# Batch 0's kv products on 64-row by 128-column TensorE tiles, and f32 warm-up products

## The chip, the cores and the metric

The kernel runs on one core of one Trainium2 chip. The metric is the device time of one execution in microseconds. The engines are TensorE (PE, with PEld for its weight loads), VectorE (DVE), ScalarE (ACT), GpSimd (POOL) and SyncE (SP). Each engine takes its instructions in the order of its own queue and waits at an instruction until its semaphores are met. SP issues the plain loads and stores; POOL issues the loads that cast f32 to bf16.

## The reference, cut to what matters

```python
# q, k, v: (8 batches, 8 heads, 576 rows, 64)
q_s = softmax(q, over the 64 columns)
k_s = softmax(k, over the 576 rows)
kv  = einsum('bhsd,bhse->bhde', k_s, v)        # 64 x 64 for each head
attn = einsum('bhsd,bhde->bhse', q_s, kv)
x = attn, heads side by side                    # (4608, 512)
h = x @ w_in                                    # (4608, 2048)
s = sin(alpha * h)
out = (h + s * s / (alpha + 1e-9)) @ w_out      # (4608, 512)
```

The kernel takes exp(k) without dividing it; a column of ones beside v gives the sum of each column of exp(k) in the same product, and kv is divided by that sum once.

## The kernel before, in words

The 4608 rows of x are handled in nine slices of 512 columns of xT (x transposed, bf16). A slice t needs the attention of a batch; then 16 steps h (four products of 128x128 weights by 512 columns each, `mm_h`, L261), each followed by a sine (ACT, L267), a square (ACT, POOL or DVE by a list of letters, L269 to L273) and a sum (DVE, L277) that gives g; then 64 products with w_out (`mm_o`, L281). The order on every engine is written out by hand.

Heads lie in SBUF in this way: the 128 partitions hold two halves e of 64 rows; a head is h = 2*ii + x inside a half, so `ii` chooses a pair of heads and `x` one of the pair. `kv_mm` (L162 to L175) makes kv for a pair: for each of nine j, each x and each e one product with 64 rows, 64 weight columns (exp(k) of one head) and 65 moving columns (v of that head and its column of ones), so 36 products per pair, in four TensorE quarters. The result for the two heads x lies in the two halves of the partitions of `kvp`, one PSUM bank per e. `kv_norm` (L177 to L184) takes the reciprocal of the sums (L182, 128x2) and multiplies (L183, 128x128 for one pair, 128x256 for two) into `kbd`. `attn_x` (L211) multiplies kv with the transposed q.

The opening is the part that the change touches (L367 to L408). Its orders are:

- PE: seven warm-up products (`warm_up(7)`, L372: bf16 identity by 512 columns of `qe`, result never read), eight transposes of q for pair 0 into `tp0`, two warm-up products, the 36 kv products of pair 0, one warm-up product, the transpose of alpha, eight transposes of q for pair 1, `attn_x` of pair 0, the 36 kv products of pair 1, three products of h, `attn_x` of pair 1 (into `lp`), five products of h, and then the steps of slice 0, whose first waits for a part of w_in.
- ACT: exp of q pair 0 in two halves, exp of k pair 0, exp of q pair 1 in two halves, the cast of v pair 0 (`vb`), the copy of `tp0` into `qT`, exp of k pair 1, the copy of alpha, two copies into xT (L396), one more (L405), a load of the sine table (L406), and then the sines.
- DVE: sums, reciprocal and product for q of pair 0 and pair 1 (L362 to L364), the kv norm of pair 0, two casts of v pair 1 (L331), the copy of the second transposes into `qT` (L391), the kv norm of pair 1, the reciprocal of alpha, one copy into xT (L405), and then the sums L277.
- SP loads q, k and v of batch 0 without waiting. POOL issues two parts of v, eight loads of w_in (L107) and two of w_out (L110) one after another, and waits for nothing that PE does.

Later loads are tied to this order. In slice 0, after the sum of step 6, DVE writes one element into the tile of q (L443) and SP then loads the first half of q of batch 1 (L444). After steps 8 and 10 POOL issues two loads of w_out. After step 12 the second half of q, and then k and v of batch 1 (L452) follow. POOL issues the last part of w_out once k of batch 1 has landed. In the middle of the w_out products of slice 0 PE makes kv of batch 1: pair 0 (39.18 us) and pair 1 (42.65 us); in between a DVE write (L514) lets SP load a small part of q (`q8`, L515) and all of batch 2 (L98).

`late_q8` (L534) uses the kv of batches 0 and 1 once more at step 15 of slice 1.

Of the kernel before, what the change touches and what calls it, by code (L numbers as in the profile page):

```python
# [15 lines left out]
F32 = mybir.dt.float32  # L16
BF16 = mybir.dt.bfloat16
AX = mybir.ActivationFunctionType
ALU = mybir.AluOpType
# [4 lines left out]
def kernel(  # L24
# [14 lines left out]
    nc = tc.nc  # L39
    ctx.enter_context(nc.allow_non_contiguous_dma(reason="layout"))  # L40
    B, H, S, D = q.shape
# [3 lines left out]
    J = 9  # L45
    P = S // J
# [8 lines left out]
    singles = ctx.enter_context(tc.tile_pool(name="singles", bufs=1))  # L55
# [3 lines left out]
    small = ctx.enter_context(tc.tile_pool(name="small", bufs=2))  # L59
# [6 lines left out]
    ident = singles.tile([128, 128], F32, name="ident")  # L66
    identb = singles.tile([128, 128], BF16, name="identb")
# [4 lines left out]
    alpha_rows = singles.tile([nN, 128], F32, name="alpha_rows")  # L72
    alpha_sb = singles.tile([128, nN], F32, name="alpha_sb")
    inva_sb = singles.tile([128, nN], F32, name="inva_sb")
    kbd = [singles.tile([128, 2, 2, D], BF16, name=f"kbd{n}") for n in range(2)]
    vb = [singles.tile([128, J, 4 * 65], BF16, name=f"vb{n}") for n in range(2)]

# [7 lines left out]
    staged = {}  # L85
# [27 lines left out]
    A = {}  # L113
# [10 lines left out]
    def exp_half(name, b, ii, j1=J, j0=0):  # L124
        if (name + "e", b) not in A:
            A[name + "e", b] = att2.tile([128, J, 4 * D], BF16, name=name + "e")
        exp_to(A[name + "e", b][:, j0:j1], staged[name, b][:, :, j0:j1], (ii,))
# [34 lines left out]
    def kv_mm(b, ii, pool, split=False):  # L162

        if ii == 0 or split:
            A["kvp", b] = pool.tile([128, 2, 512], F32, name="kvp", tag="a")
        kvp, ke, vt = A["kvp", b], A["ke", b], vb[b % 2]
        for j in range(J):
            for x in range(2):
                h = 2 * ii + x
                for e in range(2):  # L170
                    r = slice(64 * e, 64 * e + 64)
                    nc.tensor.matmul(kvp[64 * x:64 * x + 64, e, ii * 65:(ii + 1) * 65],  # L172
                                     ke[r, j, h * 64:(h + 1) * 64],
                                     vt[r, j, h * 65:(h + 1) * 65],
                                     start=(j == 0), stop=(j == J - 1))  # L175

    def kv_norm(b, i0=0, i1=2):  # L177

        kt, m = kbd[b % 2], i1 - i0
        kvr = small.tile([128, 2, 2], F32, name="kvr")[:, :, 0:m]  # L180
        src = A["kvp", b][:, :, i0 * 65:i1 * 65].rearrange("p e (ii c) -> p e ii c", ii=m)
        nc.vector.reciprocal(kvr, src[:, :, :, D])  # L182
        nc.vector.tensor_tensor(kt[:, :, i0:i1], src[:, :, :, 0:D],  # L183
                                kvr.unsqueeze(3).to_broadcast([128, 2, m, D]), op=ALU.mult)  # L184
# [26 lines left out]
    def attn_x(b, ii, j0, j1, outs):  # L211

        for e in range(2):
            for x in range(2):
                r = slice(64 * x, 64 * x + 64)
                nc.tensor.matmul(outs[x][64 * e:64 * e + 64], kbd[b % 2][r, e, ii],  # L216
                                 A["qT", b][r, ii, j0:j1, e * 64:(e + 1) * 64], start=True, stop=True)

    def x_cols(b, j0, j1):
# [11 lines left out]
    def last_j(b, xn):  # L231

        for ii in range(2):
            attn_x(b, ii, J - 1, J, [xn[:, x, ii * P:(ii + 1) * P] for x in range(2)])
# [12 lines left out]
    def bank(kind):  # L247

        if kind == "k":
            return ps_k.tile([128, 2, MF], F32, name="kvp", tag="a")[:, 0]  # L250
        pool = {"a": lambda: ps_h[0], "b": lambda: ps_h[1], "l": lambda: ps_l, "o": lambda: ps_o[0], "p": lambda: ps_o[1]}[kind]()
        return pool.tile([128, MF], F32, name={"l": "lp", "o": "op", "p": "op"}.get(kind, "hp"), tag=kind)
# [69 lines left out]
    ps_k = ES.enter_context(tc.tile_pool(name="ps_k", bufs=1, space=PSUM, reuse_waits="tile"))  # L322

    tp0 = ps_h[0].tile([128, 8, 128], BF16, name="tp", tag="a")
    warm = ps_h[0].tile([128, 4, 128], F32, name="warm", tag="a")
# [19 lines left out]

    def warm_up(n):

        for _ in range(n):
            nc.tensor.matmul(warm, identb, A["qe", 0][:, 0:4, 0:128], start=True, stop=True)  # L349

# [4 lines left out]
    def norm_q0(ii):  # L357

        part = qs0[:, 0:8, 2 * ii:2 * ii + 2]
        src = qe0[:, 0:8, ii * 128:(ii + 1) * 128].rearrange("p j (x d) -> p j x d", x=2)  # L360
        for j0 in (0, 4):
            nc.vector.tensor_reduce(part[:, j0:j0 + 4], src[:, j0:j0 + 4], axis=AXL.X, op=ALU.add)  # L362
        nc.vector.reciprocal(part, part)
        nc.vector.tensor_tensor(qn0[:, ii, 0:8].rearrange("p j (x d) -> p j x d", x=2), src,  # L364
                                part.unsqueeze(3).to_broadcast([128, 8, 2, D]), op=ALU.mult)
# [3 lines left out]
    exp_half("k", 0, 0)  # L369
    for j0 in (0, 4):  # L370
        exp_half("q", 0, 1, j0 + 4, j0)
    warm_up(7)  # L372
    norm_q0(0)
    norm_q0(1)
    q_tile(0)
# [1 line left out]
    cast_v0(0, 0, 9, ACT_CP)  # L377
    ACT_CP(A["qT", 0][:, 0, 0:8], tp0)
    exp_half("k", 0, 1)
    warm_up(2)  # L380
    kv_mm(0, 0, ps_k, split=True)
    warm_up(1)
    tpa = warm[:, 0, 0:nN]
    nc.tensor.transpose(tpa, alpha_rows, ident[0:nN, 0:nN])
    kv_norm(0, 0, 1)
    tp1 = ps_l.tile([128, 8, 128], BF16, name="tp", tag="l")
    q_transpose_ii(0, 1, 0, 8, tp1)
    ACT_CP(alpha_sb, tpa)
# [3 lines left out]

    xp = [bank("b") for _ in range(2)]
    attn_x(0, 0, 0, 8, xp)
    for x in range(2):
        ACT_CP(xT[:, 2 * x, 0:MF], xp[x])  # L396
    kv_mm(0, 1, ps_k, split=True)
    kv_norm(0, 1, 2)
    nc.vector.reciprocal(inva_sb, alpha_sb)
    for ni, ki in ((0, 0), (1, 0), (0, 1)):  # L400
        mm_h(0, ni, ki, ki + 1)
    xp = [bank("l") for _ in range(2)]
    attn_x(0, 1, 0, 8, xp)
    for x in range(2):
        (ACT_CP, DVE_CP)[x](xT[:, 2 * x + 1, 0:MF], xp[x])  # L405
# [32 lines left out]
    with ES:  # L438
# [70 lines left out]
        take(os, 10)  # L509
        kv_mm(1, 0, ps_k, split=True)  # L510
        kv_norm(1, 0, 1)
        transpose_q1(1, DVE_CP)
        for b in range(2):
# [20 lines left out]
        def late_q8(ni):  # L534
            if ni == 11:
                tp = ps_k.tile([128, 2, 2, 128], BF16, name="tp", tag="a")
                for b in range(2):
                    for ii in range(2):
                        nc.tensor.transpose(tp[:, ii, b], A["qe", 1][:, J - 2 + b, ii * 128:(ii + 1) * 128], identb)
                DVE_CP(A["qT", 1][:, :, J - 2:J], tp)  # L540
            elif ni == 15:
                xp = ps_k.tile([128, 2, 512], F32, name="xp", tag="a")
                for ii in range(2):
                    for b in range(2):
                        for e in range(2):
                            for x in range(2):
                                r, c = slice(64 * x, 64 * x + 64), (2 * ii + b) * P
                                nc.tensor.matmul(xp[64 * e:64 * e + 64, x, c:c + P], kbd[b][r, e, ii],
                                                 A["qT", 1][r, ii, J - 2 + b, e * 64:(e + 1) * 64],
                                                 start=True, stop=True)  # L550
                DVE_CP(xT[:, :, 16 * P:18 * P].rearrange("p (x i) n -> p x i n", x=2),
                       xp[:, :, 0:4 * P].rearrange("p x (i n) -> p x i n", i=2))

        for ni in range(nN):
            h_slot(1, ni, SQ[ni], lag)
            flush(lag, 1)
            late_q8(ni)
# [34 lines left out]
    for ii in range(2):  # L592
        xp = [bank("ab"[ii]) for _ in range(2)]
# [29 lines left out]
    for ni in range(nN):  # L623
# [4 lines left out]
        elif ni in (9, 13):  # L628
            ii = ni // 12
# [3 lines left out]
    for t in range(3, nT):  # L633
        b = t + 1 if t + 1 < B else None
# [74 lines left out]
```

## Time and profile before

| | |
|---|---|
| median of 3 runs | 283.23 us (282.95 to 283.6) |
| profiled execution | 282.79 us, span 281.0 us |
| PE busy | 267.7 us (95%) |
| ACT, DVE, POOL busy | 223.8, 185.5, 81.3 us |
| first product of PE | 4.98 us |
| PE's wait for w_in in the opening ends | 14.87 us |
| PE's wait for v of batch 1 ends | 42.65 us |

The span is the profiled part of the execution; 1.8 us of it lie around the span. Times in the text are microseconds from the start of the span. In a line of the timeline the first number is the start, the second the length of the whole group, then come engine, source line, operation, output and inputs, tile and form, the count, and in brackets how long the engine had been idle before and what ended that.

### The profile page before, as it was taken

Reading aid. Unit: us, or ns where it says so; the run is one execution under the profiler, and the core shown is the slowest. Engines: PE = TensorE matmul, PEld = TensorE weight load, DVE = VectorE, ACT = ScalarE, POOL = GpSimd, SP = SyncE. Lnnn points to the kernel's source line nnn. Section 1 sums busy time; section 2 is a strip of 40 time slices with the busy share of each in tenths; the row PEclk is TensorE's granted clock in tenths of the full one; section 3 lists DMA queues with packets and bytes.
Section 4 is the critical chain, followed back from the end, with each engine's and each line's share of the span. In section 5 each row is a group of like instructions: output and inputs, shape, how many; then the busy total and the mean of one; then the engine's idle time right before and its main releaser. Section 6 shows DMA issues by size and latency. Waiting matters only on the chain.

```text
span 281.0 us, 4925 instructions
## 1 busy us (share of the span) xinstructions
PE 267.7 (95%) x1890; PEld 124.0 (44%) x1919; DVE 185.5 (66%) x279; ACT 223.8 (80%) x322; POOL 81.3 (29%) x77
## 2 busy tenths in 40 slices
PE   2899989999999999999999999999999999999994
PEld 1444444444443444444444444444444444444443
DVE  3968776899878767766776677577775555555412
ACT  5899458999588999899989998999877777777400
POOL 2968121777667460205003500350000000000000
PEclk9999999999999999999999999999999999999999
DMA  7999999997599039712991199125011111111143
GB/s 263 299 194 232 278 307 319 361 343 253 120 229 399 2 81 334 290 37 48 267 383 45 37 263 392 38 50 124 8 29 40 37 37 37 40 41 42 40 106 75
DMA packets 39320, 45.82 MB, mean 163 GB/s; under 512 B 17008, under 2 KB 22656, under 8 KB 39296
## 3 DMA queue, kind: packets, MB, share of 16 engines
q1 hardware_dynamic: 33392, 40.58, 46.9%
q0 software_dynamic: 5744, 4.79, 10.3%
q8 instruction: 15, 0.25, 0.3%
q10 hardware_dynamic: 160, 0.13, 0.2%
q14 instruction: 9, 0.07, 0.1%
HBM read 36.71 MB, written 9.44 MB: 164 GB/s over the span
## 4 chain that ended last, share of the span: by engine, by line
PE 85%; DMA 8%; POOL 2%; issue 1%; SPq 1%; ACT 1%; DVE 1%; ACTq 0%
PE op L281 38%; PE hp L261 38%; DMA st_v<-in_v_dram 4%; DMA win<-in_moe_w_in_dram 2%; PE lp L261 2%; PE kvp L172 2%; DMA st_k<-in_k_dram 2%; PE op L261 1%; PE op L679 1%; POOL s L271 1%; PE kvp L261 1%; PE hp L216 1%; PE xp L216 1%; POOL st_v L306 1%; DVE g L277 1%
## 5 line engine op out<-in xcount | busy, mean ns | idle before, releaser
L277 DVE SCALAR_TENSOR_TENSOR g<-s,inva_sb,hp 128x512 bf16<-128x512 f32 x128 | 94.5, 746 | 58.7 <-ACT s L269 53.3
L261 PE MATMUL hp<-xT,win 128*128 128x512 bf16 x506 | 127.7, 379 | 0.6 <-PE lp L216 0.2
L281 PE MATMUL op<-wout,g 128*128 128x512 bf16 x478 | 121.0, 379 | 1.6 <-issue 1.1
L267 ACT ACTIVATE s<-hp,alpha_sb 128x512 f32<-128x512 f32 x128 | 86.1, 682 | 22.3 <-PE hp L261 21.0
L261 PEld LDWEIGHTS <-win 128*128 128x128 bf16 x576 | 55.7, 98 | 67.8 <-DMA win<-in_moe_w_in_dram 1.2
L281 PEld LDWEIGHTS <-g 128*128 128x128 bf16 x560 | 53.4, 98 | 64.8 <-issue 2.3
L269 ACT ACTIVATE s<-s 128x512 f32<-128x512 f32 x112 | 70.5, 630 | 3.5
L271 POOL TENSOR_TENSOR s<-s 128x512 f32<-128x512 f32 x29 | 30.1, 1053 | 17.6 <-ACT s L267 11.3
L151 POOL TENSOR_TENSOR qn<-qe,qs 128x1152 bf16<-128x1152 bf16 x11 | 23.2, 2127 | 29.5 <-DVE qs L145 24.4
L293 DVE COPY o<-op 128x512 f32<-128x512 f32 (+2 forms) x33 | 21.8, 661 | 10.2 <-PE op L281 7.9
L136 POOL CAST vb<-st_v 128x1152 bf16<-128x1152 f32 x12 | 14.7, 1257 | 45.6 <-DMA st_v<-in_v_dram 45.6
L117 ACT ACTIVATE qe<-st_q 128x1152 bf16<-128x1152 f32 (+2 forms) x18 | 17.7, 1025 | 6.1 <-DMA st_q<-in_q_dram 6.0
L117 ACT ACTIVATE ke<-st_k 128x1152 bf16<-128x1152 f32 x16 | 17.9, 1151 | 3.2 <-DMA st_k<-in_k_dram 3.2
L144 DVE TENSOR_REDUCE qs<-qe 128x36 f32<-128x2304 bf16 x5 | 12.8, 2551 | 8.3 <-ACT qe L117 8.3
L117 ACT ACT_TABLE_LOAD x7 | 9.0, 1283 | 0.8 <-PEq L693 0.7
L172 PE MATMUL kvp<-vb,ke 64*64 64x65 bf16 x576 | 6.9, 194 | 2.2 <-ACT vb L470 1.5
L349 PE MATMUL warm<-qe,identb 128*128 128x512 bf16 x10 | 4.1, 554 | 5.0 <-ACT qe L117 5.0
L281 PE MATMUL hp<-wout,g 128*128 128x512 bf16 x31 | 8.6, 379 | 0.1
L172 PEld LDWEIGHTS <-ke 64*64 64x64 bf16 x576 | 6.0, 106 | 6.1 <-issue 3.4
L281 PE MATMUL lp<-wout,g 128*128 128x512 bf16 x30 | 8.4, 379 | 0.2 <-issue 0.2
L261 PE MATMUL lp<-xT,win 128*128 128x512 bf16 x30 | 7.5, 379 | 0.1
L229 DVE CAST xT<-xp 128x1024 bf16<-128x1024 f32 (+1 forms) x7 | 7.4, 1065 | 0.0
(89 smaller groups left out, 135.8 us busy)
## 6 DMA issues: line engine op xcount, KB each, us to landing
out_dram<-o SPq DMA_DIRECT2D x70, 128.0 KB, 2.4
st_q<-in_q_dram SPq DMA_DIRECT2D x6, 1152.0 KB, 6.3
st_k<-in_k_dram SPq DMA_DIRECT2D x6, 1152.0 KB, 8.6
st_v<-in_v_dram SPq DMA_DIRECT2D x6, 1152.0 KB, 11.3
st_k<-in_k_dram SPq DMA_DIRECT2D x4, 576.0 KB, 8.1
st_q<-in_q_dram SPq DMA_DIRECT2D x4, 512.0 KB, 6.0
st_v<-in_v_dram SPq DMA_DIRECT2D x3, 576.0 KB, 10.0
wout<-in_moe_w_out_dram POOLq DMA_DIRECT2D x3, 512.0 KB, 12.7
```

Of the source, the lines that this page charges most:

```text
L117: nc.scalar.activation(dst[:, :, ii * 128:(ii + 1) * 128].rearrange("p j (x d) -> p x j d", x=2), src[:, ii::2], AX.Exp)
L136: engs[ii](vv[:, 2 * ii:2 * ii + 2, :, 0:D], staged["v", b][:, ii::2])
L144: nc.vector.tensor_reduce(qs, A["qe", b].rearrange("p j (i d) -> p j i d", i=4), axis=AXL.X, op=ALU.add)
L151: engs[ii % len(engs)].tensor_tensor(qn[:, ii, 0:j1].rearrange("p j (x d) -> p j x d", x=2), qe[:, ii], part.unsqueeze(3).to_broadcast([12 ...
L172: nc.tensor.matmul(kvp[64 * x:64 * x + 64, e, ii * 65:(ii + 1) * 65], ke[r, j, h * 64:(h + 1) * 64], vt[r, j, h * 65:(h + 1) * 65], start= ...
L261: nc.tensor.matmul(hp, win[:, KO[k], ni * 128:(ni + 1) * 128], xT[:, KO[k], t * MF % NX:t * MF % NX + MF], start=(k == 0), stop=(k == 3))
L267: nc.scalar.activation(s, hp, AX.Sin, scale=alpha_sb[:, ni:ni + 1])
L269: nc.scalar.activation(s, s, AX.Square)
L271: nc.gpsimd.tensor_tensor(s, s, s, op=ALU.mult)
L277: nc.vector.scalar_tensor_tensor(G[t][:, ni], in0=s, scalar=inva_sb[:, ni:ni + 1], in1=hp, op0=ALU.mult, op1=ALU.add)
L281: nc.tensor.matmul(acc, G[t][:, ni, j * 128:(j + 1) * 128], wout[:, ni, :], start=(ni == 0), stop=(ni == nN - 1))
L293: eng(o[:, cols], acc)
```

## The change

Three things are changed, all for batch 0:

- The kv products of a pair are made by `kv0_mm`: for each j and e one product with 64 rows, all 128 weight columns of the pair, and 130 moving columns (both heads' v and ones). That is 18 products for a pair; the blocks of one head's k with the other head's v are made too and not used.
- The norm `kv0_norm` takes one column of sums per e (128x2) and multiplies 128 x (2 e, 2 blocks, 64) into a new tile `kv0`, from which `attn_x` and `late_q8` read the blocks that they need through `kv_of`.
- The warm-up products have the f32 identity as weights and the staged f32 q as moving operand, of n columns. They wait for the load of q and the identity in place of exp(q). The first seven become four of 512 columns, the two become one of 256, and the one becomes one of 128.

```diff
+    kv0 = singles.tile([128, 2, 2, 2, D], BF16, name="kv0")
...
+    def kv0_mm(ii):
+
+        A["kvp", 0] = ps_k.tile([128, 2, 512], F32, name="kvp", tag="a")
+        for j in range(J):
+            for e in range(2):
+                r = slice(64 * e, 64 * e + 64)
+                nc.tensor.matmul(A["kvp", 0][:, e, 0:130], A["ke", 0][r, j, ii * 128:(ii + 1) * 128],
+                                 vb[0][r, j, ii * 130:(ii + 1) * 130], start=(j == 0), stop=(j == J - 1))
+
+    def kv0_norm(ii):
+
+        kvr = small.tile([128, 2], F32, name="kvr0")
+        src = A["kvp", 0][:, :, 0:130].rearrange("p e (x c) -> p e x c", x=2)
+        nc.vector.reciprocal(kvr, src[:, :, 0, D])
+        nc.vector.tensor_tensor(kv0[:, :, ii], src[:, :, :, 0:D],
+                                kvr.unsqueeze(2).unsqueeze(3).to_broadcast([128, 2, 2, D]), op=ALU.mult)
+
+    def kv_of(b, x, e, ii):
+        r = slice(64 * x, 64 * x + 64)
+        return kbd[b % 2][r, e, ii] if b else kv0[r, e, ii, x]
...
-                nc.tensor.matmul(outs[x][64 * e:64 * e + 64], kbd[b % 2][r, e, ii],
+                nc.tensor.matmul(outs[x][64 * e:64 * e + 64], kv_of(b, x, e, ii),
                                  A["qT", b][r, ii, j0:j1, e * 64:(e + 1) * 64], start=True, stop=True)
...
     def warm_up(n):
 
-        for _ in range(n):
-            nc.tensor.matmul(warm, identb, A["qe", 0][:, 0:4, 0:128], start=True, stop=True)
+        nc.tensor.matmul(warm.rearrange("p a b -> p (a b)")[:, 0:n], ident,
+                         staged["q", 0][:, 0, 0:8].rearrange("p j d -> p (j d)")[:, 0:n], start=True, stop=True)
...
-    warm_up(7)
+    for _ in range(4):
+        warm_up(512)
     norm_q0(0)
     norm_q0(1)
     q_tile(0)
...
-    warm_up(2)
-    kv_mm(0, 0, ps_k, split=True)
-    warm_up(1)
+    warm_up(256)
+    kv0_mm(0)
+    warm_up(128)
     tpa = warm[:, 0, 0:nN]
     nc.tensor.transpose(tpa, alpha_rows, ident[0:nN, 0:nN])
-    kv_norm(0, 0, 1)
+    kv0_norm(0)
...
-    kv_mm(0, 1, ps_k, split=True)
-    kv_norm(0, 1, 2)
+    kv0_mm(1)
+    kv0_norm(1)
...
-                                nc.tensor.matmul(xp[64 * e:64 * e + 64, x, c:c + P], kbd[b][r, e, ii],
+                                nc.tensor.matmul(xp[64 * e:64 * e + 64, x, c:c + P], kv_of(b, x, e, ii),
```

## The prediction

> **What bounds the kernel now.** I read the chain of waits first, up to 46 us (columns: start, length, what):
>
> ```profile
> 8.90 5.92 DMA win<-in_moe_w_in_dram
> ...
> 14.87 1.90 PE hp L261 x8
> ...
> 29.41 12.43 DMA st_v<-in_v_dram
> ...
> 41.86 0.75 ACT vb L470
> ...
> 42.65 0.48 PE kvp L172 x32
> ```
>
> PE waits for a load twice: for w_in until 14.87, for v of batch 1 until 41.84 (cast, then product at 42.65). From there on the chain is PE almost without a break. So an opening that is quicker gains nothing by itself, and one that is later by d costs d less what the second wait swallows. The timeline of PE gives the room at both:
>
> ```profile
> 4.98 3.15 PE L349 MATMUL warm<-qe,identb 128*128 128x512 bf16 x7 [4.98 <-ACT qe L117]
> 7.92 0.87 PE L199 MATMUL tp<-identb,qn 128*128 128x128 bf16 x8
> 8.63 0.59 PE L349 MATMUL warm<-qe,identb 128*128 128x512 bf16 x2
> 9.72 0.48 PE L172 MATMUL kvp<-vb,ke 64*64 64x65 bf16 x36 [0.50 <-ACT vb L331]
> 10.45 0.23 PE L384 MATMUL warm<-ident,alpha_rows 16*128 16x16 f32 x1
> 13.20 0.41 PE L216 MATMUL lp<-qT,kbd 64*64 64x512 bf16 x4
> ...
> 39.18 0.48 PE L172 MATMUL kvp<-vb,ke 64*64 64x65 bf16 x36 [0.22 <-ACT vb L470]
> ...
> 42.65 0.48 PE L172 MATMUL kvp<-vb,ke 64*64 64x65 bf16 x36 [1.24 <-ACT vb L470]
> ```
>
> At 14.87 there is no room: five products of h begin at 13.77 and, at 0.216 each, end at 14.85, and w_in lands at 14.82. Between 14.87 and 39 PE runs with no gap. At 39.18 it waits 0.22 and at 42.65 1.24, so 1.46 us of lateness disappear there. The rows also show the clock. The granted clock reads 1.00 throughout, yet the weight loads of the first seven products start 0.43 apart (0.833 ns per column) and the eight transposes take 0.107 each, while the two products at 8.63 are 0.21 apart (0.42 ns per column). PE reaches full speed at about 8.6, 3.6 us after its first product.
>
> Third, the windows (DMA share is the next to last column):
>
> ```profile
> 27.00:28.00 1.00, 1.00 (x6) 0.49 (x5) 0.81 (x3) 1.00 (x3) 0.65 (x2) 1.00 1.14 291
> 28.00:29.00 1.00, 1.00 (x7) 0.42 (x5) 1.00 (x3) 0.98 (x2) 0.97 (x1) 1.00 1.17 252
> ...
> 40.00:41.00 1.00, 0.95 (x7) 0.34 (x5) 0.97 (x4) 0.51 (x1) 0.00 (x0) 1.00 1.05 201
> 41.00:42.00 1.00, 0.41 (x5) 0.22 (x5) 0.57 (x2) 0.79 (x2) 0.11 (x1) 1.00 0.25 47
> ```
>
> No slice from 4 to 41 us is below 1.00. The transfers always have work ahead of them, so a load issued later need not land later.
>
> **The change part by part.** All durations are of the profiled execution (282.79 us, 0.44 under the median); the difference is then added to the median, 283.23.
>
> *First warm-up.* The seven products (3.15 us, ended at 8.1 with the first transpose already at 7.92) go. Four f32 products come, and begin with the load of q, which ACT's exp takes at 4.30; I say 4.35, 0.63 earlier. No row shows an f32 product of 512 columns. The nearest are the bf16 one (factor 1) and the f32 transpose of alpha, L384: 229 ns for 16 columns. The line through the bf16 rows (194 ns at 65 columns, 379 at 512) is 167 ns plus 0.414 per column; L384 lies 62 ns above 167, 3.9 ns per column, factor 9.4 if all of it were per column. The middle by ratio is 3.1. I take 4, above it, since L384 shares type and identity operand with the new products. That is 4 x 512 x 4 = 8192 column steps. Up to 8.6 they go at 0.833 ns (5100 done), the other 3090 at 0.42 (1.30 us): the stream ends at 9.90. Their weight loads are part of the instruction; bf16 hides them wholly, L384's load took 0.133. Sixteen of those bare would be 2.1 us; I take a quarter, 0.5. End: 10.4. The transposes of q, ready at 7.84, wait until then. At factor 1 the stream would end at 6.1 and delay nothing; at 9.4 near 14.5 (19250 steps), which is nearly 5 us more.
>
> The page FP8 and Floating Point Precision of the Trainium skill (TensorE Precision Notes) states that true f32 takes four passes through the array; by it the factor would be 4 and the estimate the same, against factor 1 that a count of instructions would suggest.
>
> *Clock.* The one opening that a row shows is at 8.6. If it follows the first product by 3.6 us it comes at 8.0 now, and the stream ends at 10.15. The page TensorE: Matmul & The Clock Gate (The HAM clock gate) says that a free-running window of about 3.4 us must be busy, so an earlier start need not open the clock earlier; by that rule it comes anywhere from 7.8 to 11.2, the row's 8.6 lying inside.
>
> *Other warm-ups.* Two bf16 products (0.43) become 256 columns: 4 x 256 x 0.42 = 0.43. One (0.21) becomes 128 columns, 0.21. Bounds by the same factors: a quarter of that, and 2.4 times.
>
> *Path to kv of pair 0.* After 10.4: eight transposes 0.45 (weight loads of the second group at 10.61), warm-up 0.43, and 0.1 between them: the kv products start at 11.4 in place of 9.72, +1.66. The cover that ACT's cast of v gave (ended 9.67) is gone. ACT's copy of tp0 moves from 9.57 to about 11.0, and exp of k pair 1, the alpha copy and the xT copies queue behind it; each is still ready before its user below.
>
> *kv products.* 36 in 0.48 become 18. A quarter now makes nine in 0.29, 0.032 each: 65 x 0.42 and 5 ns. With both row halves side by side, nine pairs of 130 x 0.42 + 5 = 0.059 make 0.53, with the tail 0.19 0.72: +0.24. Lower bound 0; upper, halves in turn, 18 x 0.057 + 0.19 = 1.2, +0.74. I take +0.24, as the four quarters of L172 and of `attn_x` (four in 0.41) do run side by side. Pair 1's products stay hidden behind DVE.
>
> *Norm.* The same tile's rows show both sizes:
>
> ```profile
> L182 DVE RECIPROCAL kvr<-kvp x10: 154/173/177, 10.4 to 193.2; 128x4 f32<-128x4 f32 x6, 128x2 f32<-128x2 f32 x4
> L183 DVE TENSOR_TENSOR kbd<-kvp,kvr x10: 291/424/426, 10.6 to 193.5; 128x256 bf16<-128x256 f32 x6, 128x128 bf16<-128x128 f32 x4
> ```
>
> So 0.424 for 0.291: +0.13 for each pair. DVE runs without a gap from 10.45 to 13.29 (norm, casts, copy, norm), and the second norm releases `attn_x` into `lp` at 13.20. Both +0.13 lie on the path.
>
> *Sum.* `lp` is later by 1.66 + 0.24 + 0.26 = 2.16. Behind it queue the copies into xT at 13.66, ACT's table load at 14.26 and the first sine (15.66), the five h products and the step at 14.87. With no room there, slice 0 shifts by 2.16, on PE and on ACT, which is full from 15.55 to 28.43. At 39.18 and 42.65 1.46 is swallowed. Left: +0.70.
>
> *Loads that move.* Tied to slice 0 and issued 2.16 later: both halves of q1 (SP L444, 22.29 and 27.46), two w_out (POOL L110, 23.89), k and v of batch 1 (SP L452, 27.87 to 29.88). POOL's earlier loads do not move. By 27.87 8.40 MB had been issued and 6.9 MB moved (the sum of the windows), 1.5 MB ahead, 5 us at 0.29 MB per us: no starvation, so I cost the landing at 41.84 at nothing; if that cover were false it would be up to +2.16. `q8` (SP L515, 41.02, landing up to 3.0 us later, used at 45.13) and batch 2 (SP L98 at 42.04, used by ACT at 62.03) move by 1.9; batch 2 has 10 us of room, `q8` 0.7, and what it delays ACT by, 1.2, meets ACT's own room of 0.45 at 56.98 and the PE shift of 0.7.
>
> *Nothing:* `attn_x` and `late_q8` read blocks of the same size; `kv0` is a tile of its own, no wait. The PE's first weight load no longer waits on DVE, which was 3 us early.
>
> Total: 283.23 + 0.70 = 283.9.
>
> **Rivals.** (1) *Swallowed.* If the f32 loads hide (0) and the clock opens at 8.0, the stream ends at 9.65, d is 1.41, under 1.46: 283.2. For it: the bf16 rows hide theirs. Between, each 0.1 is 0.1; 282.7 to 283.8 within 0.2% (0.57 us, about what a measurement tells from no change). (2) *The clock stays shut* through the stream: 8192 x 0.833 = 6.8, end 11.2, then transposes 0.86, warm-up 0.85, kv about 1.0: d about 4.5, +3: 286.3. Against: products without gaps opened it before. (3) *Loads follow their issue*: landing +2.16, 285.4. Against: the windows. (4) *Faster.* The runs shown reach 0.81 above the profiled execution. If that is executions whose clock opens late after only 3 us of warm-up, a stream of twice the length that starts 0.63 earlier ends them: -0.4 to -0.8, 282.6. It decides if the stream's end is before about 9.7, so that the second wait still covers. Against: that same room of 1.46 already hides most of a late clock.
>
> **How the numbers follow.** Chances: my sum 0.39 (283.6 to 284.4), swallowed 0.33, clock shut 0.06, loads late 0.08, faster 0.14. Slower 0.53, same 0.33, faster 0.14. The range 282.7 to 285.2 leaves out the shut clock, half of the late loads and half of the faster case, 0.17. The factor 9.4 (288) has under 0.02 and lies outside.
>
> **What will show it.** In the timeline of PE after: warm-up from 4.35 to about 10.4 (9.65 for rival 1, 11.2 for 2); transposes then, not at 7.92; kv group of 0.7 at 11.4; L183's successor 0.42 twice; first sine near 17.8; PE at 14.87 moved to 17.0; the idle time ahead of the kv products at 42.65 gone, with them at 43.35. If that idle time is still there and the cast of v begins at 41.86, rival 1 holds; if the cast begins later, rival 3. I am wrong if f32 products cost far from four bf16 ones, if the first wait is not for `lp`, or if the halves take turns.

## The result and the profile after

The changed kernel takes 283.86 us (median of 22 runs, 282.47 to 285.5) and the kernel before 282.61 us (22 runs, 281.86 to 284.51). The ratio is 1.0037, with a 95% interval of 1.0024 to 1.005: slower by about 1.05 us, inside the range 282.7 to 285.2 and on the forecast side. The profiled execution of the changed kernel (283.29 us, span 281.2) is one of its quicker ones; the median span of the 22 is 282.0.

The timeline of PE of the changed kernel, first the opening and then the stretch of the second wait (start, length, engine, line, operation, count, idle time before):

```profile
4.55 5.09 PE L370 MATMUL warm<-st_q,ident 128*128 128x512 f32 x8 [4.55 <-DMA st_q<-in_q_dram]
9.48 0.61 PE L221 MATMUL tp<-identb,qn 128*128 128x128 bf16 x8
9.93 0.65 PE L370 MATMUL warm<-st_q,ident 128*128 128x256 f32 x2
10.51 0.68 PE L184 MATMUL kvp<-vb,ke 64*128 64x130 bf16 x18
14.23 0.41 PE L238 MATMUL lp<-qT,kv 64*64 64x512 bf16 x4
...
39.51 0.35 PE L173 MATMUL kvp<-vb,ke 64*64 64x65 bf16 x20
40.03 0.32 PE L173 MATMUL kvp<-vb,ke 64*64 64x65 bf16 x16 [0.16 <-POOL vb L493]
42.06 0.48 PE L173 MATMUL kvp<-vb,ke 64*64 64x65 bf16 x36
...
55.97 0.38 PE L562 MATMUL tp<-identb,qe 128*128 128x128 bf16 x4 [0.72 <-DVE g L299]
```

The stream of f32 products is there; each product has two records, so four make eight. `lp` comes at 14.23 in place of 13.20, 1.03 later. The wait ahead of the kv products at 42.65 is gone. But those products are not late: they start at 42.06, 0.59 *earlier* than before, since v of batch 1 had landed 0.58 sooner in this execution (its cast starts at 41.28 in place of 41.86). PE loses that lead, and more, between 44 and 56: a new wait of 0.72 stands at 55.97, ahead of transposes that started at 55.70 before.

The timeline of ACT says why. First the line of before, then those of the changed kernel:

```profile
45.13 0.74 ACT L117 ACTIVATE qe<-q 128x256 bf16<-128x256 f32 x2
```

```profile
45.42 0.72 ACT L118 ACTIVATE qe<-q 128x256 bf16<-128x256 f32 x2 [0.73 <-DMA q<-in_q_dram]
46.16 1.28 ACT L548 ACT_TABLE_LOAD   x1
```

This is the exp of `q8`, the last thing that ACT does before it loads the sine table for slice 1. In the profile of before ACT did not wait for that load. Now ACT is ready sooner, at 44.69, and then waits 0.73 for it. Slice 1's sines start 0.27 later and the span is 0.2 longer.

### The profile page after: what moved, and what is told of

It is laid out like the page before. It is cut to its first block, busy times and chain, and to the rows that moved or that the text cites. A ratio compares the mean times of both kernels' runs of the same rounds, so it can differ in the third digit from the quotient of the medians.

```text
span 281.2 us, 4857 instructions
## 1 busy us (share of the span) xinstructions
PE 269.7 (96%) x1856; PEld 125.4 (45%) x1885; DVE 185.7 (66%) x279; ACT 224.1 (80%) x322; POOL 82.0 (29%) x77
## 4 chain that ended last, share of the span: by engine, by line
PE 81%; DMA 4%; issue 4%; POOL 3%; DVE 3%; ACT 3%; SPq 0%; POOLq 0%; ACTq 0%
PE op L303 38%; PE hp L283 35%; DMA st_v<-in_v_dram 3%; POOL s L293 3%; PE warm L370 2%; ACT s L289 2%; DVE g L299 2%; PE kvp L173 2%; DMA st_q<-in_q_dram 1%; PE op L283 1%; PE op L702 1%; POOL vb L493 1%; PE hp L238 1%; PE xp L238 1%; DVE vb L353 0%
## 5 line engine op out<-in xcount | busy, mean ns | idle before, releaser
L118 ACT ACTIVATE qe<-st_q 128x1152 bf16<-128x1152 f32 (+2 forms) x18 | 17.7, 1025 | 6.0 <-DMA st_q<-in_q_dram 5.8
L370 PE MATMUL warm<-st_q,ident 128*128 128x512 f32 (+2 forms) x12 | 6.2, 653 | 4.5 <-DMA st_q<-in_q_dram 4.5
L173 PEld LDWEIGHTS <-ke 64*64 64x64 bf16 x504 | 5.0, 106 | 3.5 <-issue 1.3
L299 DVE SCALAR_TENSOR_TENSOR g<-s,inva_sb,lp 128x512 bf16<-128x512 f32 x8 | 5.8, 742 | 0.9 <-POOL s L293 0.9
```

What stands on the lines that cost most here:

```text
L118: nc.scalar.activation(dst[:, :, ii * 128:(ii + 1) * 128].rearrange("p j (x d) -> p x j d", x=2), src[:, ii::2], AX.Exp)
L299: nc.vector.scalar_tensor_tensor(G[t][:, ni], in0=s, scalar=inva_sb[:, ni:ni + 1], in1=hp, op0=ALU.mult, op1=ALU.add)
L370: nc.tensor.matmul(warm.rearrange("p a b -> p (a b)")[:, 0:n], ident, staged["q", 0][:, 0, 0:8].rearrange("p j d -> p (j d)")[:, 0:n], sta ...
```

## The experiments

In the table, "exp of q8" is the start of that line in the timeline of ACT, and the last column is the span less that start. The order is that of the runs.

| kernel | ratio to before (95%) | exp of q8, us | waited for q8, us | span, us | span less start |
|---|---|---|---|---|---|
| before | 1 | 45.13 | 0 | 281.0 | 235.87 |
| the change | 1.0037 (1.0024 to 1.005) | 45.42 | 0.73 | 281.2 | 235.78 |
| e1, kv and norm alone | 1.0019 (1.0005 to 1.0032) | 45.37 | 0.68 | 281.2 | 235.83 |
| e2, f32 warm-up alone | 1.003 (1.0012 to 1.0047) | 45.66 | 0.18 | 281.6 | 235.94 |
| e3, change, q8 at 31 us | 1.0026 (1.001 to 1.0042) | 45.45 | 0 | 281.3 | 235.85 |
| e4, before, q8 at 30 us | 1.0025 (1.001 to 1.004) | 45.61 | 0 | 281.4 | 235.79 |
| e5, change, q8 two us sooner | 1.0009 (0.9991 to 1.0028) | 46.19 | 0 | 282.0 | 235.81 |
| e6, before, q8 two us sooner | 0.9988 (0.9975 to 1.0001) | 45.53 | 0 | 281.3 | 235.77 |
| e7, change, two products | 1.0018 (1.0001 to 1.0034) | 44.97 | 0.52 | 280.8 | 235.83 |
| e8, change, eight products | 1.0152 (1.0132 to 1.0173) | 49.84 | 1.00 | 285.7 | 235.86 |
| e9, the change again | 1.003 (1.0012 to 1.0048) | 45.81 | 0.37 | 281.6 | 235.79 |
| e10, change, q8 by POOL | 1.0009 (0.9994 to 1.0023) | 44.71 | 0 | 280.5 | 235.79 |
| e11, before, q8 by POOL | 1.0002 (0.9985 to 1.0019) | 44.54 | 0 | 280.4 | 235.86 |
| e12, two products, q8 by POOL | 0.9994 (0.9979 to 1.0009) | 45.34 | 0 | 281.2 | 235.86 |

The last column is the main finding. In fourteen profiled executions of thirteen kernels the span ends 235.77 to 235.94 us after the exp of q8 begins, although that start itself moves by 5.3 us. So what these kernels differ in inside the span has been decided when that instruction starts.

The time of an execution is its span and what lies around it, and both are on record for every execution, not only for the profiled ones. The second table has the means (in brackets half of a 95% interval; before's spans are those of the same chip).

| kernel | mean span less that of before, us | mean time around the span, us |
|---|---|---|
| before | 0 | 1.78 |
| the change | about +0.8 (estimate) | 1.96 |
| e1, kv and norm alone | +0.02 (0.28) | 2.27 |
| e2, f32 warm-up alone | +0.72 (0.40) | 1.79 |
| e3, change, q8 at 31 us | +0.69 (0.40) | 1.85 |
| e4, before, q8 at 30 us | +0.62 (0.38) | 1.80 |
| e5, change, q8 two us sooner | +0.03 (0.52) | 1.95 |
| e6, before, q8 two us sooner | -0.39 (0.34) | 1.80 |
| e7, change, two products | +0.33 (0.36) | 1.94 |
| e8, change, eight products | +4.36 (0.70) | 1.81 |
| e9, the change again | +0.65 (0.48) | 2.04 |
| e10, change, q8 by POOL | -0.02 (0.36) | 2.03 |
| e11, before, q8 by POOL | -0.05 (0.44) | 1.78 |
| e12, two products, q8 by POOL | -0.42 (0.23) | 2.12 |

For the change the spans of before beside it are not on record; the estimate takes before's mean time there, 282.79, less 1.78.

The last column separates the two forms of the kv products. With the old form (before, e2, e4, e6, e11) the time around the span is 1.73 to 1.85 us in all 147 executions on record. With the new form it is over 2.2, and up to 3.0, in 22 of 110. Three of these 22 were profiled: e1 (2.59), e9 (2.31) and e12 (2.97). Their traces, and no others, show a packet of 16 KB on a DMA queue of kind "instruction" that starts 1.7 to 2.2 us after the last instruction. Counted from that instruction it lands at 2.83, 2.54 and 3.21, in each case 0.23 or 0.24 more than the time around the span. In before the last such packet starts at 268.6, inside the span; so it does in e3 and e8 (276.7 and 278.9), where no execution is over 2.2. The new form has 18 products for a pair in place of 36. That the shorter program is what moves the packet is an inference; no run varied the length alone.

### The two parts alone: e1 and e2

e1 keeps `kv0_mm` and `kv0_norm` and puts the warm-up back; e2 is the reverse.

```diff
# e1, against the changed kernel
-    for _ in range(4):
-        warm_up(512)
+    warm_up(7)
-    warm_up(256)
+    warm_up(2)
-    warm_up(128)
+    warm_up(1)
# and the body of warm_up as before: bf16 identity, 512 columns of exp(q)
```

> Batch 0's kv and norm in the new form, the warm-up products as before. Theory A (the lateness of the opening decides, whatever makes it): kv group about 0.7 us in place of 0.48, L183's successor 0.42, lp later by 0.3 to 0.4 us; all swallowed by the waits at 39.18 and 42.65 and by the loads of w_in in slice 0, so the time is that of before within 0.1%. Theory B (the kv form itself costs, in a place that the opening's path does not show): a ratio of 1.002 to 1.004.

> The f32 warm-up products alone, kv and norm as before. Theory A: the stream of four ends at 9.5 to 10.2, lp later by 0.6 to 1.3 us, most of it swallowed: ratio 1.000 to 1.002. Theory C (the f32 stream is the whole cost): the ratio of the full change, 1.0037.

Measured were 1.0019 and 1.003, so theory A misses both times. In e1 its mechanism holds all the same: `lp` came at 13.77, 0.57 later than before, and the spans are those of before (+0.02), so the lateness was swallowed. The 0.19% lies around the span. Theory B, a cost of the kv form in a place that the opening does not show, is borne out by that, though the place is behind the last instruction. In e1's profile ACT also stood still for 0.68 before the exp of q8 (the profile puts this wait down to a DVE copy that the exp does not read; the load of q8, released at 41.2 in place of 40.85, is what it reads). But ACT was ready at 44.69, sooner than before's 45.13, and the wait does not show in the mean span.

In e2 it is the other way round: +0.72 in the span and nothing around it, which is what theory C said within the interval. The sum of both ratios, 0.49%, agrees with the 0.37% of the change within the intervals.

e2 also shows the clock. Its stream starts at 4.61, and its transposes come only at 10.84, 1.36 later than in the profile of the change; `lp` follows at 15.29, 2.09 later than before, where 0.6 to 1.3 was expected.

### q8 issued much sooner: e3 and e4

```diff
             for ii in range(2):
                 for n, t in (("k", k), ("v", v)):
                     nc.sync.dma_start(out=staged[n, 1][:, ii::2]...
+            for b in range(2):
+                nc.sync.dma_start(out=q8[:, :, b], in_=src_view(q, b)[:, :, 8 * D:J * D])
...
-        for b in range(2):
-            DVE_CP(q8[:, 0, b, 0:1], zero)
-            nc.sync.dma_start(out=q8[:, :, b], in_=src_view(q, b)[:, :, 8 * D:J * D])
-        load_batch(2)
+        load("q", q, 2, gate=DVE_CP)
+        load("k", k, 2)
+        load("v", v, 2)
```

> The changed kernel, with the small load q8 moved: SP issues it right behind the loads of k and v of batch 1, and batch 2's loads are held by a DVE write into the tile of q instead of the write into q8. Theory D (the lateness reaches the end by way of q8: DVE write 0.70 later, q8 0.70 later, exp of q8 and first sine of slice 1 0.27 later): ACT no longer waits for q8, the first sine of slice 1 comes at 47.0 or sooner, and the time falls by 0.3 us or more, to before's or below it. Theory E (PE is late through slice 0 and the second wait no longer covers it): the time stays 1.0037 of before.

> The kernel before, with the same move of q8. It is the control for the move itself: ACT did not wait for q8 in the profiled execution of before, so by theories D and E alike the time is that of before within 0.1%. If it is faster by 0.2% or more, the q8 load was a bound of before as well, in executions that the profile does not show.

The control e4 failed its expectation by 0.25%, so the move is not neutral and this pair settles nothing about q8 by its times. The timelines of PE show what it did. First e3, then e4:

```profile
43.42 1.02 PE L303 MATMUL hp<-wout,g 128*128 128x512 bf16 x4 [0.96 <-DMA wout<-in_moe_w_out_dram]
```

```profile
43.59 1.02 PE L281 MATMUL hp<-wout,g 128*128 128x512 bf16 x4 [1.01 <-DMA wout<-in_moe_w_out_dram]
```

PE waits a microsecond for the last part of w_out, which it does in no other profile. In the windows of before the transfers are full until about 41 us, so the reading that the early load pushed this one out lies near; beyond the two rows nothing shows it. What the pair does show is that the two kernels cost the same within their intervals (1.0026 and 1.0025) once something other than q8 is last.

### q8 issued two microseconds sooner: e5 and e6

Here the DVE write that releases q8 stands ahead of the kv products of pair 0 in DVE's order instead of behind them; batch 2's loads stay where they were.

```diff
         q1_norm(1)
+        for b in range(2):
+            DVE_CP(q8[:, 0, b, 0:1], zero)
+            nc.sync.dma_start(out=q8[:, :, b], in_=src_view(q, b)[:, :, 8 * D:J * D])
         take(os, 10)
# and the old place as in e3
```

> The changed kernel, with the load q8 issued two microseconds sooner (its DVE write stands behind the product q1_norm of pair 1, at about 39.5, in place of 41.55), and batch 2's loads held at their old place by a DVE write into their own tile. Theory D (q8 ties the lateness to the start of slice 1's sines): the exp of q8 starts at 44.7 to 45.1 in place of 45.42, and the time falls by 0.3 to 0.7 us against the full change, to a ratio of 1.000 to 1.002. Theory E (something else in the opening): the ratio of the full change, 1.0037. Both allow a wait for the last part of w_out at the products ahead of it, as where q8 was issued at 31; if it appears, exp of q8 starts later by as much.

> The kernel before with the same move of q8 to about 39.3, as the control. Theory D: exp of q8 starts where PE and ACT allow, 45.1 as in before, since q8 was there in time: ratio 1.000, or 0.999 where q8 was late in some executions. If w_out waits as it did with q8 at 30, ratio 1.001 to 1.0025.

The changed kernel falls to 1.0009, and the control to 0.9988: theory D's expectation holds for the times. The start that was expected for e5 (44.7 to 45.1) was missed, since this execution had the clock opening late: the DVE write stood at 41.63, no sooner than the 41.55 of the change, and only its place in the order was moved. Its timelines:

```profile
9.13 2.29 PE L370 MATMUL warm<-st_q,ident 128*128 128x512 f32 x3
11.26 0.61 PE L221 MATMUL tp<-identb,qn 128*128 128x128 bf16 x8
15.91 0.41 PE L238 MATMUL lp<-qT,kv 64*64 64x512 bf16 x4
...
45.13 0.41 PE L238 MATMUL hp<-qT,kbd 64*64 64x512 bf16 x4
...
46.19 0.73 ACT L118 ACTIVATE qe<-q 128x256 bf16<-128x256 f32 x2
```

The stream ends at 11.26 and `lp` is 2.71 later than before. ACT does not wait for q8 any more; it is PE's `attn_x` at 45.13 (44.06 before) that is late. So there are two ways from the opening to the exp of q8, by the q8 load and by PE, and PE's own way counts where the delay is large.

### The length of the stream: e7 and e8

```diff
-    for _ in range(4):
+    for _ in range(2):      # e7; range(8) in e8
         warm_up(512)
```

> The changed kernel with two f32 products of 512 columns in the first warm-up in place of four. Theory A (length of the stream, with the clock's opening, sets the lateness): the stream ends at about 8.0, the kv products of pair 0 start at 9.7 to 10.0, lp is later than before by 0.3 to 0.7, exp of q8 starts at 45.1 to 45.4; ratio 1.000 to 1.002. Theory F (the shorter stream leaves the clock shut for longer, as little work is done per time): the products stay at 0.83 ns per column past 10 and lp is as late as in the full change; ratio 1.003 or more.

> The changed kernel with eight f32 products of 512 columns in place of four. Theory A, with the room used up: four more products at full speed are 4 x 0.86 = 3.4 us; kv of pair 0 starts near 13.9, lp near 17.7, and nothing more is swallowed behind it, so the time rises by 3.0 to 3.5 us against the full change, ratio 1.014 to 1.017. If the loads' landing still hid part of it, the rise is under 2.5 us.

Eight products cost 1.0152. Against the change's 1.0037 that is 1.15% or 3.2 us, where 3.0 to 3.5 was expected for four more products at full speed. With the room used up, the delay goes through nearly one to one. In e8's profile the clock opened near 10 only, `lp` stands at 18.90 (17.7 was expected) and ACT waits 1.00 for q8. Two products cost 1.0018, the same ratio as the bf16 warm-up with the new kv (e1), though here part of it may lie in the span (+0.33, 0.36). The products ended by 8.3, the transposes still ran at half speed, and the clock opened between 9 and 10. Theory F fails: `lp` comes at 13.48, 0.28 later than before.

### q8 released by a load and not by PE: e9 to e12

The last four ran on one chip. In e10, e11 and e12 the write that releases q8 is on POOL, behind its cast of v, so that it follows a load and no lateness of PE or DVE.

```diff
         cast_v1(0)
+        for b in range(2):
+            GP_CP(q8[:, 0, b, 0:1], zero)
+            nc.sync.dma_start(out=q8[:, :, b], in_=src_view(q, b)[:, :, 8 * D:J * D])
# and the old place as in e3
```

> The changed kernel as it is, beside the next three on one chip, and a second profiled execution of it. In all ten profiles so far the span is the start of the exp of q8 (the first of the two at line 118 or 117 that read the tile q) plus 235.8 us within 0.1. Theory D: that holds here too, and the place of this execution in it is given by when the products of the first warm-up go to 0.42 ns per column: an opening near 10 to 11 us means a start near 46, one near 7 to 8 a start near 45.4. Ratio 1.002 to 1.005.

> The changed kernel with q8 released by a POOL write behind POOL's cast of v pair 0 of batch 1 (39.2 to 40, set by the load of v and not by PE or DVE), batch 2's loads held as before. Theory D: ACT does not wait for q8, the exp of q8 starts when ACT is ready (44.7 where the clock opened at 7.3); ratio 1.000 to 1.002, and what is left is PE's own lateness where the clock opens late. Theory E: 1.0037.

> The kernel before with the same move: the control. Theory D: 0.998 to 1.000, as with the DVE write at 39.0 (0.9988).

> The changed kernel with two f32 products of 512 columns in the first warm-up and q8 released by POOL. With two products alone the exp of q8 waited 0.52 us for q8 at 44.97. Theory D: without that wait it starts near 44.5, the time falls by up to 0.5 us from 1.0018 of before to 0.999 to 1.001. If the kv form cost by another way than the start of slice 1's sines, it stays at 1.0018.

On this chip the change costs 1.003 and, with q8 released by POOL, 1.0009; the control is at 1.0002. The profiles of e10 and e11 make the cleanest pair of the study, e10 first:

```profile
14.87 0.41 PE L238 MATMUL lp<-qT,kv 64*64 64x512 bf16 x4
...
42.22 0.51 PE L173 MATMUL kvp<-vb,ke 64*64 64x65 bf16 x36
...
44.71 0.72 ACT L118 ACTIVATE qe<-q 128x256 bf16<-128x256 f32 x2
```

```profile
13.37 0.41 PE L216 MATMUL lp<-qT,kbd 64*64 64x512 bf16 x4
...
42.03 0.48 PE L172 MATMUL kvp<-vb,ke 64*64 64x65 bf16 x36 [0.54 <-ACT vb L470]
...
44.54 0.73 ACT L117 ACTIVATE qe<-q 128x256 bf16<-128x256 f32 x2
```

The opening of e10 is 1.50 later than that of e11, and slice 1 starts 0.17 later, the span is 0.1 longer. The kv products of pair 1 come only 0.19 later: waits for loads that e11 has, 0.54 of them in the row shown, are gone in e10. So the loads swallow the lateness, as the prediction had it, once q8 does not hang on it. The means say the same: e10's span is that of before (-0.02), e9's is 0.65 longer, and the time around the span is alike (2.03 and 2.04).

In e9 the change waits 0.37 for q8 and starts at 45.81, though its clock opened near 7.9; 45.4 was expected. There v of batch 1 landed later (ACT's cast at 42.02), which moves the start as well. Theory D's rule of the 235.8 us holds, its rule for the clock alone does not. In e12 the exp of q8 was expected near 44.5 and started at 45.34 without a wait for q8; there too ACT's cast of v was late (42.03).

e12 is at 0.9994, e6 at 0.9988: no version is faster than the kernel before beyond its interval. Their spans are shorter, by 0.42 and 0.39, just beyond the intervals; in e12 the time around the span takes most of it back.

## Why the prediction was right, point by point

**Forecast and size.** Slower by 0.70 us was predicted, 1.05 (0.7 to 1.4) measured. The forecast and the range hold. The way that was given for it, PE late by 0.70 behind the second wait, is not the way it went: in the profile PE is 0.59 early there. Of the measured 1.05 about 0.8 lies in the span, by way of q8, and nearly 0.2 around it, where the prediction had no term. That the sum came so near is in part luck.

**The price of an f32 product: right.** Factor 4 was taken between 1 and 9.4; no row of before shows it, so the choice was in part lucky. In the timeline of weight loads of the changed kernel the halves of a product lie 0.85 apart with the clock shut and 0.43 with it open, so 1.71 and 0.86 us for a product, four times the bf16 rows. The page FP8 and Floating Point Precision of the Trainium skill (TensorE Precision Notes) states four passes; these runs agree.

```profile
5.53 0.34 PEld L370 LDWEIGHTS warm<-st_q,ident 128*128 128x128 f32 x1 [0.52 <-issue]
6.38 0.34 PEld L370 LDWEIGHTS warm<-st_q,ident 128*128 128x128 f32 x1 [0.52 <-issue]
7.24 0.28 PEld L370 LDWEIGHTS warm<-st_q,ident 128*128 128x128 f32 x1 [0.52 <-issue]
7.76 0.19 PEld L370 LDWEIGHTS warm<-st_q,ident 128*128 128x128 f32 x1 [0.24 <-issue]
8.19 0.19 PEld L370 LDWEIGHTS warm<-st_q,ident 128*128 128x128 f32 x1 [0.24 <-issue]
```

**The weight loads: 0.5 us too much.** 0.854 for half a product is 1024 columns at 0.833 ns with nothing left over. The loads are hidden wholly; their term was 0.

**The clock: mis-sized.** 8.6 was taken for its opening. The rows above put it near 7.4 in the changed kernel. By the same spacing it came near 7.9 in e9, near 8.2 in e3 and e10, near 10 in e2 and e8, and in e5 not before 10. So it does not come at a fixed time, nor at a fixed time after the first product, which starts at 4.46 to 4.75 in all of them. The page TensorE: Matmul & The Clock Gate (The HAM clock gate) describes a free-running window of about 3.4 us; the spread of these openings is about as wide as that, and it agrees better than either reading of the single row that I had. It does not fit wholly: in the changed kernel the clock opened 2.9 after the first product, sooner than a whole such window and than the 7.8 worked out from it. The stream of four products ended between 9.48 and 11.26 for that reason, around the predicted 10.4.

**kv and norm: right.** 0.68 was measured for 0.72 predicted, and the two norms took 0.42 each:

```profile
11.44 0.42 DVE L192 TENSOR_TENSOR kv<-kvp,kvr 128x256 bf16<-128x256 f32 x1
...
13.75 0.42 DVE L192 TENSOR_TENSOR kv<-kvp,kvr 128x256 bf16<-128x256 f32 x1
```

**The lateness of `lp`: 2.16 predicted, 1.03 in the profiled execution,** 1.21 in e9, and 2.71 in e5 with the late clock. Over the five profiles of the change with four products (the change, e3, e5, e9, e10) the mean is 1.60: the sum was about 0.5 too large, as much as its term for the weight loads. Behind it slice 0 took up 0.3 more than I allowed (its first w_out product at 27.75 in place of 27.02, 0.73 later). The weight loads show where. The first two lines are of before, the third is of the changed kernel:

```profile
13.54 0.76 PEld L261 LDWEIGHTS <-win 128*128 128x128 bf16 x5 [0.23 <-issue]
14.87 2.06 PEld L261 LDWEIGHTS <-win 128*128 128x128 bf16 x11 [0.57 <-DMA win<-in_moe_w_in_dram]
```

```profile
14.57 2.49 PEld L283 LDWEIGHTS <-win 128*128 128x128 bf16 x13 [0.23 <-issue]
```

Before, the five products of h begin with the load at 13.54 (the record of the first product is missing) and not at 13.77, so at 0.216 each they end at about 14.63 and PE waits 0.24 for w_in until 14.87. "No room" at 14.87 was a misreading. In the changed kernel the loads run on without a wait.

**The room at the second wait: right, and yet not decisive.** PE's idle time ahead of the products at 42.65 went, as predicted, though they came at 42.06 and not at 43.35, and e10 beside e11 shows that 1.5 us of lateness leave 0.1 in the span.

**The step that failed** is the one on `q8`, which I let pass: "what it delays ACT by, 1.2, meets ACT's own room of 0.45 at 56.98 and the PE shift of 0.7". That its DVE write moves was seen, if not the size (41.55 in place of 40.85, and not 1.9 later). But the idle time at 56.98 is no room, and in the profile PE had no shift to hide the wait behind. The idle time is in every one of the profiles, wherever slice 1 starts: 0.45 to 0.47 where ACT did not wait for q8, 0.55 or 0.56 in the six where it did. Behind the exp of q8 nothing is ever taken up; the column of 235.8 us shows that.

In both ways of freeing q8 the ratio fell to 1.0009 and the mean span came back to that of before (+0.03 and -0.02); with two products it fell from 1.0018 to 0.9994. So q8's release accounts for the change's cost inside the span, 0.2 to 0.3% of the whole. The neighbouring intervals overlap, and the size is rough. The 0.09% that is left agrees with the time around the span, 0.17 and 0.25 longer than before's. Whether q8 also holds back some executions of the kernel before is open: the move shortened the control's span in e6 (-0.39) and not in e11 (-0.05).

**The rivals.** *Swallowed* was right for PE and wrong for the time. *Loads follow their issue* did not happen at this size: issued one microsecond later, v landed no later than before in the profile. For large delays it happens in part: in e8 the loads are issued 5.7 later and ACT's cast of v starts at 44.78, 2.9 later. *Clock shut* came nearest in e5, without staying so to the end (its parts add up to a d of about 4.1, not 4.5). *Faster* has nothing for it: an opening past 10 comes with the longer stream too (e5), and with the stream at half its length, e7, the time is no better than that of before.

## What to carry to other kernels

When a long wait for data seems to swallow a delay, list every transfer whose release depends on the delayed work, and follow each one to its first reader: a small load can carry the delay around the wait. Idle time on a later engine counts as room only if it gets shorter when something arrives late, and that can be looked up by comparing the same gap in two executions. A load that is released by a write of a busy engine inherits that engine's lateness; released by another load's arrival it does not, but issued far too early, as in e3 and e4, it can cost as much by another wait. And where a tenth of a per cent counts, compare the spans of all executions as well as their times: a part of the cost can lie behind the last instruction, where no timeline of an engine shows it.

## What was not expected of the hardware

The cast of v on POOL (128x512) took 0.62 us in e2, e3 and e10, 0.72 before, 1.22 in e1 and 1.54 in the change. It grows with the time that it lies beside DVE's product `q1_norm`, a broadcast multiply of bf16 tiles in SBUF, where that product began first: 0.62 becomes 0.48 and the whole overlap (1.07 in the change, 0.74 in e1). The changed kernel's timeline has the two together:

```profile
38.29 1.21 DVE L513 TENSOR_TENSOR qn<-qe,qs 128x1024 bf16<-128x1024 bf16 x1
38.43 1.54 POOL L493 CAST vb<-st_v 128x512 bf16<-128x512 f32 x1 [0.44 <-DMA st_v<-in_v_dram]
```

In e2 that product started at 39.13, when the cast that began at 38.54 was nearly over. Where the cast began first and the product came upon it, the cast keeps its 0.62 and the product is the longer one: 1.41 in e3, 1.51 in e5 and 1.30 in e10, in place of 1.21. In these rows the one that begins second waits. So a DVE that is late by a microsecond moved onto POOL's cast and held the second half of the kv products, which wait for POOL at 40.03 in the change. That the two share something is read from these rows alone; no run separated it.

Also, the granted clock reads 1.00 in all windows of before, while the spacing of products is that of half speed until 7.4 to 10 us; in the opening the clock has to be read from the spacing.
